# Feed-forward transposes by DMA in a four-layer forward and backward kernel

## The chip, the cores and the metric

The kernel runs on one core of a Trainium2 chip. The core has a matrix engine (TensorE, PE in the profile), a vector engine (VectorE, DVE), an activation engine (ScalarE, ACT), a general engine (GpSimd, POOL) and a queue engine that issues transfers (SyncE, SP). Sixteen DMA engines move data between the chip's memory (HBM) and the on-chip memory (SBUF). TensorE writes to PSUM, a small memory of eight banks. The metric is the device time of one execution in microseconds (us): 1243.02 us before, the median of three runs from 1242.3 to 1243.65.

## The reference

Two blocks are applied twice, in turn, to a sequence of 2048 rows of 512 numbers: a linear attention block A (32 heads of 16) and a gated feed-forward block B of width 1376. The kernel returns the output and the gradients of the input and of all weights.

```python
def _B_ref(x, w_gate, w_up, w_down):
    g = jnp.einsum("bsd,df->bsf", x, w_gate)
    u = jnp.einsum("bsd,df->bsf", x, w_up)
    h = _sigmoid(g) * u
    return jnp.einsum("bsf,fd->bsd", h, w_down)

x = A_x
x = x + _A_ref(_layernorm(x, axis=-1), A_wqkv, A_wo)
x = x + _B_ref(_layernorm(x, axis=-1), B_w_gate, B_w_up, B_w_down)
x = x + _A_ref(_layernorm(x, axis=-1), A_wqkv, A_wo)
x = x + _B_ref(_layernorm(x, axis=-1), B_w_gate, B_w_up, B_w_down)
...
_out, _vjp = jax.vjp(_f, A_x, A_wqkv, A_wo, B_w_gate, B_w_up, B_w_down)
_grads = _vjp(grad_out)
```

## The kernel before, in words

The sequence is cut into 16 tiles of 128 rows. The layers are numbered 0 to 3; 0 and 2 are A, 1 and 3 are B. Forward, `ab_fwd` goes over the 16 tiles and does, for each, the end of an A layer and the whole of the following B layer. Backward, `b_bwd_p1` goes over the tiles of layer 3, then of layer 1; the weight gradients are summed later, in `p2_gen`, from what these loops have stored in HBM.

Forward (`ab_fwd`). For a tile, `gu` computes one of three slices (512, 512 and 352 columns of the 1376) of g and u on TensorE, the sigmoid on ACT, the gated activation hh = u x sigmoid(g) on VectorE and the derivative factor on POOL. TensorE multiplies over the partition dimension, so hh has to stand with its 1376 columns on partitions before it can be multiplied with w_down: `transposes` does this with TensorE products against the identity matrix, 11 blocks of at most 128 columns for a tile, in three groups, and ACT copies each group from PSUM to hhT. `finish` multiplies hhT by w_down (11 matmuls) and adds the result to the residual. `finish` of a tile runs late in the next tile, `after` (LayerNorm of the next layer, or storing the output) two tiles later. At a tile's end SP issues the stores of hh and of the factors `ssd`; hh, hhT and ssd have two buffers each.

Backward (`b_bwd_p1`). For a tile, `dhh_mm` multiplies the gradient (transposed to gT by `gT_make`) by w_down transposed, in three slices. `dd_ops` multiplies each slice by the two factors of `ssd` on VectorE and so gives du and dg, both in the tile dd. They are transposed as in the forward pass: `transposes` makes 22 blocks in three groups on TensorE, and ACT copies them to ddT. `dh_mm` multiplies ddT by the transposed w_up and w_gate, 22 matmuls into one PSUM bank; `LnBwd` (`ln_begin`, `sums`, `add`) does the LayerNorm's backward step. `dh_mm` of a tile runs spread through the next tile, its LayerNorm steps in the one after. `store` writes du and dg to HBM from SP at the end of the tile: two transfers of 320 KB in rows of 512 bytes (sv_hdd) and one of 48 KB in rows of 192 bytes (sv_hdl). dd, ddT and ssd have two buffers each (in layer 3 the even tiles use buffers named pre_dd and pre_ssd); dhh_ps is in a PSUM pool of two banks.

Order. The instructions of TensorE, ACT, VectorE and POOL run in the order in which the program names them (`tc.manual_schedule`). SP issues transfers in order and waits, for each, for what it reads and for its target; a waiting transfer holds up those behind it. Transfers take eight completion slots in turn, so each also waits for the transfer eight before it. In layer 3 the loads of the operands of the weight gradients (p_a, 4 MB in eight transfers) are issued together after the load of ssd for tile 8.

The lines that the text speaks of: L860 to L866 are `gu`, L874 to L879 the forward `transposes`, L886 and L888 `finish`; L996 and L997 make gT, L1004 is `dhh_mm`, L1012 `dd_ops`, L1079 to L1083 the backward `transposes`, L1101 the load of ssd, L1113 `dh_mm`, L970 to L983 `LnBwd`, L1124 and L1126 `store`.

## Time and profile before

| What | Value |
|---|---|
| Median of three runs | 1243.02 us |
| Span of the profiled execution | 1244.3 us |
| TensorE busy | 1197.8 us, 96% of the span |
| VectorE, ACT, POOL busy | 726.8, 600.7, 258.1 us |
| DMA | 256.08 MB, on average 206 GB/s |
| Forward tile, layer 1 (two in a row) | 9.18 us each |
| Backward tile, layer 1 (two in a row) | 8.53 us each |
| dd L1012, idle until dhh_ps of L1004 | 150.6 us in 45 waits |

The page gives no time of the profiled execution beside its span; the span is 1.3 us above the median of the runs. In the profile a line of the groups gives count, busy time and mean length of the instructions of one source line; in the timeline each line is a start, a length, an engine, a line and what it wrote and read. Matmuls are pipelined, so that the length of one (219 ns for a 128x128 transpose) is more than the time after which the next one starts (some 56 ns in a group of eight). The table by stretches gives, for a window of time, its length, the busy time of PE, PEld, DVE, ACT and POOL with the number of instructions, the granted clock, the busy share of the 16 DMA engines and what they moved.

### The profile page before, as it was taken

Reading aid. Unit: us, or ns where it says so; the run is one execution under the profiler, and the core shown is the slowest. Engines: PE = TensorE matmul, PEld = TensorE weight load, DVE = VectorE, ACT = ScalarE, POOL = GpSimd, SP = SyncE. Lnnn points to the kernel's source line nnn. Section 1 sums busy time; section 2 is a strip of 40 time slices with the busy share of each in tenths; the row PEclk is TensorE's granted clock in tenths of the full one; section 3 lists DMA queues with packets and bytes.
Section 4 is the critical chain, followed back from the end, with each engine's and each line's share of the span. In section 5 each row is a group of like instructions: output and inputs, shape, how many; then the busy total and the mean of one; then the engine's idle time right before and its main releaser. Section 6 shows DMA issues by size and latency. Waiting matters only on the chain. (4 is left out here: it accounts for less than half of the span.)

```text
span 1244.3 us, 22419 instructions
## 1 busy us (share of the span) xinstructions
PE 1197.8 (96%) x8646; PEld 720.2 (58%) x8646; DVE 726.8 (58%) x1410; ACT 600.7 (48%) x1105; POOL 258.1 (21%) x467
## 2 busy tenths in 40 slices
PE   8989999998999999998989999999999979999998
PEld 4445555455555555554745567755555745567777
DVE  6778886777777456664956620056664956642211
ACT  5677777557676644444626621144545616610001
POOL 4246765105665300000100010000000101200000
PEclk8999999999999999998999999999999989999999
DMA  7934455435536877858644488687767666579774
GB/s 234 300 111 166 167 182 175 167 118 182 198 137 212 280 231 240 265 168 287 227 130 144 126 287 287 175 281 216 215 201 236 172 213 182 162 245 335 238 195 147
DMA packets 266203, 256.08 MB, mean 206 GB/s; under 512 B 43248, under 2 KB 250992, under 8 KB 261232
## 3 DMA queue, kind: packets, MB, share of 16 engines
q1 hardware_dynamic: 266096, 254.65, 64.4%
q8 instruction: 67, 1.10, 0.4%
q14 instruction: 40, 0.33, 0.1%
HBM read 135.69 MB, written 118.92 MB: 205 GB/s over the span
## 5 line engine op out<-in xcount | busy, mean ns | idle before, releaser
L1309 PE MATMUL p_ps<-p_set,p_a 128*128 128x256 bf16 (+1 forms) x1792 | 186.3, 263 | 0.0
L1012 DVE TENSOR_TENSOR dd<-dhh_ps,ssd 128x512 bf16<-128x512 f32 x144 | 82.6, 629 | 157.1 <-PE dhh_ps L1004 150.6
L1309 PEld LDWEIGHTS <-p_a 128*128 128x128 bf16 x1792 | 159.0, 98 | 18.8
L1081 ACT COPY ddT<-T_ps 128x1024 bf16<-128x1024 bf16 (+1 forms) x96 | 82.9, 868 | 126.2 <-PE T_ps L1079 126.2
L866 POOL TENSOR_TENSOR ssd_t<-hh_t,oms 128x512 bf16<-128x512 bf16 (+1 forms) x96 | 101.6, 1064 | 55.0 <-ACT out_t L212 40.9
L1113 PEld LDWEIGHTS <-ddT 128*128 128x128 bf16 (+1 forms) x704 | 66.4, 98 | 70.1 <-issue 1.4
L860 PEld LDWEIGHTS <-hT 128*128 128x128 bf16 x768 | 71.6, 98 | 58.8 <-issue 1.7
L978 POOL TENSOR_SCALAR ab<-c 128x2 f32<-128x2 f32 x64 | 12.3, 192 | 448.8 <-DVE junk L975 437.5
L1288 DVE TENSOR_TENSOR dw_stg<-p_ps,dw_stg 128x512 bf16<-128x512 f32 (+2 forms) x43 | 28.3, 660 | 112.0 <-PE p_ps L1309 78.3
L860 PE MATMUL g_ps<-wg,hT 128*128 128x512 bf16 (+1 forms) x384 | 90.9, 359 | 1.2 <-DVE hT L337 1.2
L860 PE MATMUL u_ps<-wu,hT 128*128 128x512 bf16 (+1 forms) x384 | 90.9, 359 | 0.0
L865 DVE TENSOR_TENSOR hh_t<-u_ps,ssd_t 128x512 bf16<-128x512 f32 (+1 forms) x96 | 61.0, 636 | 48.3 <-PE u_ps L860 28.4
L1004 PE MATMUL dhh_ps<-wdT,gT 128*128 128x512 bf16 x372 | 83.8, 362 | 2.7 <-ACT gT L997 2.7
L1113 PE MATMUL dh_ps<-wgT,ddT 128*128 128x512 bf16 (+1 forms) x352 | 86.2, 379 | 0.0
L1113 PE MATMUL dh_ps<-wuT,ddT 128*128 128x512 bf16 (+1 forms) x352 | 81.3, 379 | 1.2 <-ACT t_sb L970 1.2
L886 PE MATMUL y_ps<-wd,hhT 128*128 128x512 bf16 (+1 forms) x352 | 81.3, 379 | 0.6 <-DVE x L888 0.6
L1297 PE MATMUL p_ps<-p_a,p_set 128*128 128x512 bf16 (+1 forms) x352 | 81.6, 383 | 0.0
L862 ACT ACTIVATE ssd_t<-g_ps 128x512 bf16<-128x512 f32 (+1 forms) x96 | 53.2, 554 | 32.8 <-PE g_ps L860 32.6
L975 DVE SCALAR_TENSOR_TENSOR junk<-t_sb,h_ld 128x512 bf16<-128x512 f32 x64 | 44.0, 687 | 39.8 <-ACT t_sb L970 39.8
L970 ACT ACTIVATE t_sb<-dh_ps,rstd_all 128x512 f32<-128x512 f32 x64 | 44.0, 687 | 38.1 <-issue 20.3
L1568 ACT CAST fin_o<-sg_ps 128x512 bf16<-128x512 f32 x4 | 2.3, 586 | 122.1 <-PE sg_ps L1566 122.1
L1290 ACT CAST dw_stg<-p_ps 128x512 bf16<-128x512 f32 (+2 forms) x43 | 24.0, 561 | 76.5 <-PE p_ps L1309 48.4
(226 smaller groups left out, 2224.2 us busy)
## 6 DMA issues: line engine op xcount, KB each, us to landing
p_set<-sv_hdd SPq DMA_DIRECT2D x30, 1024.0 KB, 6.4
sv_ssd<-ssd_t SPq DMA_DIRECT2D x32, 688.0 KB, 3.4
ssd<-sv_ssd SPq DMA_DIRECT2D x24, 688.0 KB, 5.0
sv_hdd<-dd SPq DMA_DIRECT2D x48, 320.0 KB, 3.5
sv_hdd<-hh_t SPq DMA_DIRECT2D x32, 320.0 KB, 2.6
h_ld<-sv_h SPq DMA_DIRECT2D x32, 256.0 KB, 4.4
p_set<-sv_dqk SPq DMA_DIRECT2D x8, 1024.0 KB, 5.8
p_a<-sv_h SPq DMA_DIRECT2D x12, 512.0 KB, 6.2
```

The costliest lines, as they stand in the source:

```text
L860: nc.tensor.matmul(ps[:, 0:w], lhsT=hT[:, kc, :], rhs=w_sb[:, kc, c0:c0 + w], start=(kc == 0), stop=(kc == NDC - 1))
L862: nc.scalar.activation(ssd_t[:, 0, c0:c0 + w], g_ps[:, 0:w], ACT.Sigmoid)
L865: nc.vector.tensor_tensor(hh_t[:, c0:c0 + w], u_ps[:, 0:w], ssd_t[:, 0, c0:c0 + w], ALU.mult)
L866: nc.gpsimd.tensor_tensor(ssd_t[:, 1, c0:c0 + w], hh_t[:, c0:c0 + w], oms[:, 0:w], ALU.mult)
L886: nc.tensor.matmul(y_ps[:], lhsT=T["hhT"][0:r, fc, :], rhs=k.wd[0:r, fc, :], start=(fc == 0), stop=(fc == NFC - 1))
L970: k.nc.scalar.activation(self.t[:], dh_ps, ACT.Identity, scale=rstd_col, accum_out=self.c12[:, 0:1])
L1004: k.nc.tensor.matmul(ps[:, 0:w], lhsT=gT[:, jc, :], rhs=k.wdT[:, jc, c0:c0 + w], start=(jc == 0), stop=(jc == NDC - 1))
L1012: k.nc.vector.tensor_tensor(dd[:, a, c0:c0 + w], ps[:, 0:w], ssd[:, a, c0:c0 + w], ALU.mult)
L1081: nc.scalar.copy(ddT[:, :, fcs[0]:fcs[0] + nfull, :], tps[:, :, 0:nfull, :])
L1113: nc.tensor.matmul(T["dh"][:], lhsT=T["ddT"][0:r, a, fc, :], rhs=(k.wuT, k.wgT)[a][0:r, fc, :], start=(i == 0), stop=(i == 2 * NFC - 1))
L1297: nc.tensor.matmul(ps[0:r, :], lhsT=set_t[:, st, j * P:j * P + r], rhs=g_all[:, st, :], start=(st == 0), stop=(st == NST - 1))
L1309: nc.tensor.matmul(ps[:, icl * w:(icl + 1) * w], lhsT=h_all[:, st, ic * P:(ic + 1) * P], rhs=set_t[:, st, 0:w], start=(st == 0), stop=(st ...
```

## The change

Forward: the tile hh is widened from 1376 to 1408 columns (11 x 128), POOL fills the last 32 with zeros, and for tiles 0 to 14 one DMA issued by SP, ahead of the tile's stores, transposes the whole of hh into hhT. Tile 15 keeps its transposes on TensorE. `finish` moves to the middle of the tile two later, and `after` to three tiles later.

Backward: dd is widened in the same way. For tiles 2 to 14 one DMA issued by SP, after the last slice of du and dg, transposes both into ddT (22 blocks). Tiles 0, 1 and 15 stay on TensorE. ddT has three buffers. `dh_mm` of tiles 2 to 13 runs two tiles later; those of tiles 14 and 15 run after the last tile, and in tile 3 there is none. The stores of du and dg of a tile are issued by ACT, in the next tile, after the copy of gT. The eight loads of weight-gradient operands in layer 3 are issued one a tile from tile 6 on. The mask `bdmask` becomes bf16.

```diff
@@ -25,6 +25,7 @@
...
 FLAST = F - (NFC - 1) * P
+FP = NFC * P
 FSL = [(0, 512), (512, 512), (1024, F - 1024)]
@@ -218,7 +219,7 @@
...
                 else:
-                    k.pre["dd"] = pre.tile([P, 2, F], BF16, name="pre_dd")
+                    k.pre["dd"] = pre.tile([P, 2, FP], BF16, name="pre_dd")
                     for fs in range(2):
@@ -266,8 +267,18 @@
...
 
-        ops3 = []
-        b_bwd_p1(k, 3, lambda: ops3.extend(b_operands(k, R, 3)))
+        ops3, lds3 = [], []
+
+        def mid3(st):
+            if st == 6:
+                for src, nm in ((k.sv[3]["h"], "p2_a1"), (k.sv[3]["gbf"], "p2_a2")):
+                    t = R.big.tile([P, NST, D], BF16, name=nm)
+                    ops3.append(t)
+                    lds3.extend((t[:, b * NB:(b + 1) * NB, :], dram_batch(src, b)) for b in range(NST // NB))
+            if st >= 6 and lds3:
+                o, i = lds3.pop(0)
+                nc.sync.dma_start(out=o, in_=i)
+        b_bwd_p1(k, 3, mid3)
         prectx.close()
@@ -299,7 +310,7 @@
...
                             base=0, pattern=[[-1, P]], channel_multiplier=1)
-    bdmask = consts.tile([P, P], F32, name="bdmask")
+    bdmask = consts.tile([P, P], BF16, name="bdmask")
     nc.gpsimd.memset(bdmask[:], 1.0)
@@ -897,13 +908,19 @@
...
 
-        prev = None
+        def dma_T(T):
+            T["hhT"] = wide.tile([P, NFC, P], BF16, name="hhT")
+            nc.sync.dma_start(out=T["hhT"][:], in_=T["hh"][:], transpose=True)
+
+        Ts = []
         for st in range(NST):
+            last = st == NST - 1
             hT = ln.pop(st)
...
                      ssd=wide.tile([P, 2, F], BF16, name="ssd_t"),
-                     hh=wide.tile([P, F], BF16, name="hh_t"),
-                     hhT=wide.tile([P, NFC, P], BF16, name="hhT"))
+                     hh=wide.tile([P, FP], BF16, name="hh_t"))
+            nc.gpsimd.memset(T["hh"][:, F:FP], 0.0)
+            Ts.append(T)
             nfill = fill.share(st)
@@ -912,7 +929,6 @@
...
                 gu(T, hT, 1)
-                transposes(T, 0)
                 A.attn_y(2)
@@ -921,18 +937,25 @@
...
                 A.attn_y(st + YLAG)
-                after(st - 2)
+                after(st - 3)
                 if nfill > 0:
...
                 gu(T, hT, 1)
-                transposes(T, 0)
+                if last:
+                    T["hhT"] = wide.tile([P, NFC, P], BF16, name="hhT")
+                    transposes(T, 0)
+                if st >= 2:
+                    finish(Ts[st - 2])
                 ln.stage_T(st + 1)
...
                 nc.scalar.activation(k.tab[:], k.neg[:], ACT.Exp)
-            transposes(T, 1)
+            if last:
+                transposes(T, 1)
+            else:
+                dma_T(T)
             ln.apply(st + YLAG)
@@ -941,22 +964,23 @@
...
                 fill("t", "vector")
-            if prev is not None:
-                finish(prev)
+            if last:
+                finish(Ts[st - 1])
             A.front3(st + FLAG)
...
                 fill("t" * (nfill - 1), "scalar" if st % 2 else "vector")
-            transposes(T, 2)
+            if last:
+                transposes(T, 2)
             nc.sync.dma_start(out=sv["ssd"][rows(st), :, :], in_=T["ssd"][:])
...
             nc.sync.dma_start(out=sv["hdl"][0, :, st, :], in_=T["hh"][:, NG * GW:F])
-            prev = T
+        after(NST - 3)
         if out_cb is not None:
...
             last_cb(1)
-        finish(prev)
+        finish(T)
         if out_cb is not None:
@@ -1082,14 +1106,27 @@
...
 
-        def halved(st, nm, pool):
+        def halved(st, nm, pool, w=F):
             if not first:
-                return pool.tile([P, 2, F], BF16, name=nm)
+                return pool.tile([P, 2, w], BF16, name=nm)
             if st % 2:
-                return pool.tile([P, 2, F], BF16, name=nm, bufs=1)
+                return pool.tile([P, 2, w], BF16, name=nm, bufs=1)
             if st == 0:
                 return k.pre[nm]
-            return k.pre["pool"].tile([P, 2, F], BF16, name=f"pre_{nm}")
+            return k.pre["pool"].tile([P, 2, w], BF16, name=f"pre_{nm}")
+
+        def by_dma(st):
+            return 2 <= st < NST - 1
+
+        def dd_tiles(T):
+            T["dd"] = halved(T["st"], "dd", wide, FP)
+            T["ddT"] = wide.tile([P, 2, NFC, P], BF16, name="ddT", bufs=3)
+            if by_dma(T["st"]):
+                nc.gpsimd.memset(T["dd"][:, :, F:FP], 0.0)
+
+        def dma_T(T):
+            nc.sync.dma_start(out=T["ddT"][:].rearrange("p a c t -> p (a c) t"),
+                              in_=T["dd"][:].rearrange("p a f -> p (a f)"), transpose=True)
 
@@ -1099,9 +1136,9 @@
...
                 ins = nc.sync.dma_start(out=ssd[:], in_=sv["ssd"][rows(st), :, :])
-                if mid is not None and st == 8:
+                if mid is not None:
                     with tc.issue_after(ins.ins):
-                        mid()
+                        mid(st)
             LD[st] = (ssd, hld.get(st))
@@ -1121,13 +1158,9 @@
...
             for a in range(2):
-                nc.sync.dma_start(out=sv["hdd"][1 + a, :, :, st, :].rearrange("g p w -> p g w"),
-                                  in_=dd[:, a, 0:NG * GW].rearrange("p (g w) -> p g w", g=NG))
-            nc.sync.dma_start(out=sv["hdl"][1:3, :, st, :].rearrange("a p w -> p a w"), in_=dd[:, :, NG * GW:F])
-
-        def last_transposes(T):
-            transposes(T, 2)
-            store(T)
+                nc.scalar.dma_start(out=sv["hdd"][1 + a, :, :, st, :].rearrange("g p w -> p g w"),
+                                    in_=dd[:, a, 0:NG * GW].rearrange("p (g w) -> p g w", g=NG))
+            nc.scalar.dma_start(out=sv["hdl"][1:3, :, st, :].rearrange("a p w -> p a w"), in_=dd[:, :, NG * GW:F])
 
@@ -1135,45 +1168,59 @@
...
             gT_make(0)
-        p1 = p2 = None
         load(0)
+        Ts, done = [], []
         for st in range(NST):
...
             ssd, h_st = LD.pop(st)
-            T = dict(st=st, h=h_st, ssd=ssd, dd=halved(st, "dd", wide))
-            T["ddT"] = wide.tile([P, 2, NFC, P], BF16, name="ddT")
+            T = dict(st=st, h=h_st, ssd=ssd)
+            dd_tiles(T)
+            p1 = Ts[st - 1] if st else None
+            p = p1 if st in (1, 2) else Ts[st - 2] if st >= 4 else None
+            q = done[-1] if done and not done[-1].get("end") else None
             for fs in range(2):
...
                 if st == 1 and fs == 0:
-                    last_transposes(p1)
-            if p2 is not None:
-                p2["ln"].sums()
-            if p1 is not None:
-                dh_mm(p1, 0, NFC)
+                    transposes(p1, 2)
+            if q is not None:
+                q["ln"].sums()
+            if p is not None:
+                dh_mm(p, 0, NFC)
+            if not by_dma(st):
                 transposes(T, 0)
...
             gT_make(st + 1)
-            if p1 is None:
-                transposes(T, 0)
-            else:
-                dh_mm(p1, NFC, NFC + 5)
-            if p2 is not None:
-                p2["ln"].add()
-            transposes(T, 1)
             if p1 is not None:
-                dh_mm(p1, NFC + 5, 2 * NFC)
-                ln_begin(p1)
-                last_transposes(T)
-            p1, p2 = T, p1
-        p2["ln"].sums()
-        dh_mm(p1, 0, 2 * NFC)
-        p2["ln"].add()
-        ln_begin(p1)
-        p1["ln"].sums()
-        p1["ln"].add()
+                store(p1)
+            if by_dma(st):
+                dma_T(T)
+            if p is not None:
+                dh_mm(p, NFC, NFC + 5)
+            if q is not None:
+                q["ln"].add()
+                q["end"] = True
+            if not by_dma(st):
+                transposes(T, 1)
+            if p is not None:
+                dh_mm(p, NFC + 5, 2 * NFC)
+                ln_begin(p)
+                done.append(p)
+            if st and not by_dma(st):
+                transposes(T, 2)
+            Ts.append(T)
+        store(T)
+        for p in Ts[NST - 2:]:
+            q = done[-1]
+            q["ln"].sums()
+            dh_mm(p, 0, 2 * NFC)
+            q["ln"].add()
+            ln_begin(p)
+            done.append(p)
+        p["ln"].sums()
+        p["ln"].add()
 
```

## The prediction

> **What bounds the kernel now.** First the page's busy shares.
>
> ```profile
> PE 1197.8 (96%) x8646; PEld 720.2 (58%) x8646; DVE 726.8 (58%) x1410; ACT 600.7 (48%) x1105; POOL 258.1 (21%) x467
> ...
> DMA  7934455435536877858644488687767666579774
> ```
>
> TensorE is busy nearly always; no other engine is. So work taken off TensorE is worth its own length wherever nothing else becomes later than TensorE. The second line says where that is doubtful: the DMA engines stand at 0.4 to 0.5 in the forward feed-forward (slices 3 to 13) and at 0.6 to 0.9 in the backward one (slices 15 to 18, 28 to 30).
>
> Second, the timeline of one backward tile (layer 1), in order of start (start, length, engine, line).
>
> ```profile
> 904.42 0.61 PE L1079 MATMUL T_ps<-ident,dd 128*128 128x128 bf16 x8
> 904.87 0.76 PE L1004 MATMUL dhh_ps<-wdT,gT 128*128 128x352 bf16 x4
> 905.47 0.39 PE L996 MATMUL gT_ps<-ident,gstage 128*128 128x128 bf16 x4
> 906.03 0.59 ACT L997 COPY gT<-gT_ps 128x512 bf16<-128x512 bf16 x1
> 906.77 0.61 PE L1079 MATMUL T_ps<-ident,dd 128*128 128x128 bf16 x8
> 907.21 1.46 PE L1113 MATMUL dh_ps<-wgT,ddT 128*128 128x512 bf16 x6
> 908.51 0.50 PE L1079 MATMUL T_ps<-ident,dd 128*128 128x128 bf16 x6
> 908.85 1.89 PE L1004 MATMUL dhh_ps<-wdT,gT 128*128 128x512 bf16 x8
> ```
>
> Read the starts, not the lengths, which overlap: the three transpose groups hold TensorE 0.45 + 0.44 + 0.34 = 1.23 us.
>
> Third, the busy time by stretch: two forward tiles, two backward tiles, then three short stretches inside backward tiles (last two columns: DMA share, GB/s).
>
> ```profile
> 125.00:134.18 9.18, 9.18 (x63) 4.98 (x62) 7.78 (x15) 6.67 (x13) 6.18 (x11) 1.00 0.64 216
> 134.18:143.36 9.18, 9.18 (x64) 4.96 (x62) 8.02 (x15) 6.71 (x13) 6.25 (x11) 1.00 0.45 160
> ...
> 896.34:904.87 8.53, 8.53 (x64) 4.76 (x61) 5.46 (x10) 4.03 (x7) 0.77 (x3) 1.00 0.72 218
> 904.87:913.40 8.53, 8.53 (x63) 4.78 (x61) 5.46 (x10) 4.03 (x7) 0.77 (x3) 1.00 0.70 211
> ```
>
> ```profile
> 898.55:900.75 2.20, 2.20 (x21) 1.25 (x18) 0.95 (x2) 1.53 (x2) 0.00 (x0) 1.00 1.01 281
> ...
> 910.60:911.20 0.60, 0.60 (x4) 0.27 (x3) 0.60 (x3) 0.00 (x0) 0.00 (x0) 1.00 0.97 139
> 911.60:913.40 1.80, 1.80 (x16) 1.03 (x14) 1.40 (x4) 0.00 (x0) 0.31 (x2) 1.00 0.96 364
> ```
>
> A backward tile keeps the DMA engines full for 0.71 x 8.53 = 6.06 us; a forward tile for 0.55 x 9.18 = 5.0 us. Full engines move 281 GB/s with the stores in rows of 512 bytes, about 139 while the 192-byte rows of sv_hdl go, 364 with the 5,504-byte rows of ssd.
>
> Fourth, issue to landing (us, last column).
>
> ```profile
> sv_ssd<-ssd_t SPq DMA_DIRECT2D x32, 688.0 KB, 3.4
> ssd<-sv_ssd SPq DMA_DIRECT2D x24, 688.0 KB, 5.0
> sv_hdd<-dd SPq DMA_DIRECT2D x48, 320.0 KB, 3.5
> sv_hdd<-hh_t SPq DMA_DIRECT2D x32, 320.0 KB, 2.6
> ```
>
> The same size takes 0.9 to 1.6 us longer in the backward tiles than in the forward ones.
>
> **Forward transposes.** Eleven of the 11 x 15 x 2 per tile go: the groups of 4, 4 and 3 hold TensorE 0.22 + 0.22 + 0.17 = 0.61 us a tile, 30 tiles: 18.4 us. Three ACT copies a tile go too, beside TensorE. Added: one DMA of 128x1408 (352 KB) on SP, ahead of the tile's own stores. Its result is used a tile and a half later, about 14 us, against 2.6 to 5 us for such transfers; engine time 5.0 + 1.5 = 6.5 of 8.57 us. VectorE has 7.9 us of work in that tile: if its 0.67 us of slack were gone, the gain would be too. A POOL fill of 32 columns waits until the buffer's stores of two tiles before have landed; behind it are prod and the tiny LayerNorm steps, on an engine busy 6.2 of 9.18 us: nothing taken. finish and after run a tile later; their work is the same and the last tile takes two. Taken: -18.4; ends 0 and -18.4.
>
> **Backward transposes.** 22 per tile on 13 tiles of two layers go, so TensorE's tile is 8.53 - 1.23 = 7.30 us, and 2.97 us of ACT copies go. The question is what else allows 7.30.
>
> Engines: the added DMA carries 22x128x128 bf16 = 721 KB. No row shows a transposing DMA. The bounds are the three paces above: 2.0 us of full engines at 364 GB/s, 5.2 us at 139. Its blocks are 128 elements wide, 256 bytes, between the 192-byte and the 512-byte rows; at 281 it is 2.6 us, and I take 3.0 us, a little dearer than the 512-byte row. Then a layer-1 tile needs 6.06 + 3.0 = 9.06 us of DMA engines, more than the 8.53 us it takes now.
> The Trainium skill (DMA: Bandwidth & Descriptors, Latency and other measured facts) gives 261 GB/s for one DMA-transpose kernel; by that figure the transpose would be an estimated 2.76 us, the layer-1 tile 8.82 us and the sum below about 1249; no run here shows it yet.
>
> Stores: those of tile st move from SP in tile st to ACT in tile st+1, after the gT copy. du and dg have two buffers, so the first product of tile st+2 waits for them. The ring: gT copy ends 1.75 us after the third dhh group starts (904.87 to 906.62); the third store is issued 0.93 us later (an SP row for two issues) and lands 3.2 us after that (sv_hdl row); the two products of slice 0 take 1.24 us (four in 2.48); only then has the next third dhh group its PSUM buffer. Sum 7.1 us, with the handovers about 7.3: no slack against 7.30. The transpose of the tile is issued at the same time as these stores, and they share engines; with the 1.6 us between the two 688 KB rows the ring is 8.9 us. Behind the waiting VectorE product are the rest of du/dg, LayerNorm's sums and the transpose's source; behind ACT's stores (which also wait for an earlier DMA's slot) are the read of dh and the next gT copy; behind SP's transpose, which waits for slice 2, is the load of ssd two tiles on; behind POOL's pad fill the LayerNorm scalars and the gradient cast.
>
> So a layer-1 tile: 9.05 us, 13 x 0.52 = +6.8 us. Layer 3: now 0.67 x 8.5 = 5.7 us of DMA engines (window 445 to 453.5), so five tiles follow the ring, 8.9 us: 5 x 0.37 = +1.9. In tiles 6 to 13 one 512 KB load each is issued, 1.8 us at 285 GB/s, so 5.7 + 3.0 + 1.8 = 10.5: 8 x 1.97 = +15.8. Before, these loads came in a burst that cost TensorE 1.3 us (38.67 of 40 in 480 to 520), which is got back: +16.4 for the layer.
>
> Lag: tile 3 has no dh product and one more (22 x 0.216 = 4.76 us) stands after the last tile. If the ring or the engines set the tile, tile 3 is hardly shorter. Between 0 and +4.8 a layer I take 3.0: +6.
>
> Mask in bf16: four products in all, nothing; range 0 to -1.
>
> **Sum.** The profiled execution has a span of 1244.3 us, 1.3 above the median of the runs; no row gives more around it. -18.4 + 6.8 + 16.4 + 6 = +10.8: 1255.1, less 1.3: about 1253 us. With the transpose at 5.2 us a layer-1 tile is 11.3, layer 3's are 10.9 and 12.7: +35 + 45 + 6 - 18: about 1311. At 2.0 us the engines need 8.06 and 9.5 us, ring 7.7: -6 + 3 + 6 - 18: 1228.
>
> **Rivals.** *The transposes hide (faster).* Engines hold queues full only when asked; layer-1 tiles have 2.5 us of idle engine each. If the transposing DMA is cheap and the stores have landed before it starts (ring 7.5), both layers gain about 13 x 1.0, the lag costs 3 a layer, so 1243 - 18 - 26 + 6 = about 1205; halfway, with a tile of 8.0, 1220. It decides below about 2.4 us of full engines per transpose (l-1 tile at 8.5). For it: VectorE reaches slice 2 after slices 0, 1 and the sums, so the transpose comes 1 us or so after the stores. Against: 28% idle is what is left between bursts.
>
> *The transpose is far dearer* than its bytes, in the engines or in SP's issue: from 6 us a tile the backward tiles are 12 us or more, 26 x 3.5 = +91, 1243 - 18 + 91 + 6 = about 1320. For it: 192-byte rows at half the pace. Against: one such DMA is 128 full partitions.
> The Trainium skill (VectorE: DVE Perf Modes, The three transpose paths) lists 1309 ns for a 128x128 block by DMA; were 22 blocks to go one after another, an estimated 29 us a tile, the kernel would end beyond 1700; the trace bears this out nowhere, one chance in forty within the 0.13 below.
>
> *The forward does not gain* (VectorE at 7.9 of 8.57 us): 18 us worse than the forecast, 1271.
>
> **How the numbers follow.** About 0.2% (2.5 us) is what a measurement here can tell. Slower as forecast 0.37 (own range 1246 to 1285), dearer transposes 0.13, forward without gain 0.05; hidden or half hidden 0.39; 0.06 within 0.2%, between the two. The range leaves out a tenth on each side: below 1210, above 1305.
>
> **What would show it.** the transposes of du and dg (now L1079) down from 704 to 132 matmuls; dd L1012 waiting for sv_hdd or sv_hdl instead of for dhh_ps; DMA share above 0.9 in the backward tiles; forward tiles near 8.57 us; backward tiles near 9 and 10.5. Backward tiles under 8.2 us or transposes landing in under 4 us make the forecast wrong; transposes landing after 10 us make it too low.

## The result, and the profile after

The changed kernel takes 1374.69 us (median of three runs, 1371.96 to 1375.78) against 1243.02: a ratio of 1.105, 95% interval 1.102 to 1.108. The forecast was 1253 us, range 1210 to 1305. The direction was right, the size far off.

The page of the changed kernel: TensorE's busy line, the granted clock, the DMA share.

```profile
PE 1204.8 (88%) x7744; PEld 681.9 (50%) x7744; DVE 718.9 (52%) x1410; ACT 482.6 (35%) x881; POOL 268.6 (20%) x525
...
PEclk9999988999999999999899999999989999999999
DMA  7744454643554698999965539789999666649875
```

902 matmuls are gone (8646 to 7744), yet TensorE is "busy" 7 us longer and 8 points less of the span: it waits, and in the slices where it waits its matmuls run longer. Two stretches stand out (slices counted from 0): in 3 to 13 (forward feed-forward) the DMA share is no higher than before although a transfer was added; in 16 to 19 and 27 to 30 (backward) it is at 9.

To see where the 129.8 us of span went (1374.1 against 1244.3), I cut each trace at four marks: the last feed-forward addition of layer 1 and of layer 3 (`x<-y_ps,x` on VectorE), and ACT's read of the last dh of layer 3 and of layer 1 (`t_sb<-dh_ps`). The stage called "backward 1" starts where layer 2's backward pass reads its last dh. All other stages take 7.1 us less together. The same stages take 441.4 to 449.2 us in the six kernels here that leave them as they were, and 439.2 here, so most of the 7.1 us lies within what they vary by.

| Stage, us | before | after | difference | forecast, same stage |
|---|---|---|---|---|
| forward 1 | 224.7 | 272.7 | +48.0 | -9.2 |
| forward 3 | 208.8 | 242.4 | +33.6 | -9.2 |
| backward 3 | 137.0 | 161.7 | +24.7 | +19.4 |
| backward 1 | 227.5 | 258.1 | +30.6 | +9.8 |

So 81.6 us of the loss come from the forward pass, where the forecast had a gain of 18.4.

**Forward.** The stretches of two tiles of layer 1 (columns as in the prediction's table of stretches; the last three are granted clock, DMA share, GB/s):

```profile
145.88:159.49 13.61, 10.42 (x53) 4.83 (x51) 7.64 (x15) 4.97 (x9) 6.80 (x11) 0.88 0.54 159
159.49:173.10 13.61, 10.42 (x52) 4.84 (x51) 7.63 (x15) 5.01 (x10) 6.78 (x11) 0.88 0.54 168
```

A tile takes 13.61 us instead of 9.18, TensorE works 10.42 of it, and the granted clock is 0.88 where it was 1.00. No engine and no DMA is full. The timeline of the first of these tiles shows the gap (in brackets: idle before, and what ended it):

```profile
151.81 1.25 PE L897 MATMUL y_ps<-wd,hhT 128*128 128x512 bf16 x5
...
153.71 0.76 PE L871 MATMUL u_ps<-wu,hT 128*128 128x352 bf16 x4
...
156.56 1.04 DVE L795 TENSOR_TENSOR pqnstage<-pq_all,rden_all 128x512 bf16<-128x512 bf16 x1
...
157.66 0.40 PE L341 MATMUL ln_tp<-ident,pqnstage 128*128 128x128 bf16 x4 [3.19 <-DVE pqnstage L795]
157.89 1.57 PE L871 MATMUL g_ps<-wg,hT 128*128 128x512 bf16 x4
```

and the same place of the kernel before:

```profile
128.63 2.54 PE L886 MATMUL y_ps<-wd,hhT 128*128 128x512 bf16 x11
130.05 0.90 DVE L784 TENSOR_TENSOR pqnstage<-pq_all,rden_all 128x512 bf16<-128x512 bf16 x1
131.00 0.23 PEld L330 LDWEIGHTS <-pqnstage 128*128 128x128 bf16 x4 [0.33 <-DVE pqnstage L784]
```

`front2` makes `pqnstage` on VectorE (a sum over `prod`, a reciprocal, a product), and `front3` transposes it on TensorE. Before, the 11 matmuls of `finish`, 2.54 us, stood between the two and covered that chain; what was left was a wait of 0.33 us of the weight load. The change moves `finish` to the middle of the tile. It ends at 153.06, the g and u products behind it at 154.47, and `pqnstage` is there at 157.60: TensorE stands idle for 3.19 us in this tile, and for 69.7 us in 27 such waits over both layers. The rest of the 4.4 us is slower matmuls: 10.42 us of work where 9.18 - 0.61 = 8.57 was left, at the clock of 0.88; directly after the gap a group of 4 takes 1.57 us, 4.5 us later 1.03. (3.19 of idling and 1.85 of slower work, less the 0.61 taken away, are the 4.4.)

**Backward.** DMA issues of the changed kernel (size where the profile has it, then median us from issue to landing):

```profile
ssd<-sv_ssd SPq DMA_DIRECT2D x24, 688.0 KB, 5.0
sv_hdd<-dd ACTq DMA_DIRECT2D x48, 320.0 KB, 4.3
...
sv_hdl<-dd ACTq DMA_DIRECT2D x24, 48.0 KB, 5.8
...
hhT<-hh_t SPq DMA_TRANSPOSE x30, 3.5
...
ddT<-dd SPq DMA_TRANSPOSE x19, 7.6
```

The forward transposes land after 3.5 us, and nobody waits for them. The backward ones take 7.6, and sv_hdl, the last store of a tile, takes 5.8 where it took 3.2 before the change. The timeline of the changed kernel in layer 1:

```profile
1001.86 0.59 ACT L1021 COPY gT<-gT_ps 128x512 bf16<-128x512 bf16 x1 [6.69 <-PE gT_ps L1020]
...
1002.93 0.76 ACTq L1163 DMA_DIRECT2D sv_hdl<-dd  x1
...
1003.75 5.58 SPq L1128 DMA_TRANSPOSE ddT<-dd  x1
...
1008.14 2.48 DVE L1036 TENSOR_TENSOR dd<-dhh_ps,ssd 128x512 bf16<-128x512 f32 x4 [3.44 <-DMA sv_hdl<-dd]
...
1010.70 0.59 ACT L1021 COPY gT<-gT_ps 128x512 bf16<-128x512 bf16 x1 [4.15 <-PE gT_ps L1020]
```

This is the prediction's ring, link by link: from the gT copy 1.07 us to the issue of sv_hdl, 5.21 to the product that waited for its landing, 2.56 to the next gT copy: 8.84 us, where 7.3 was worked out for stores that land undisturbed. One turn later the landing takes 8.2 us and the tile 13.95. Tiles 2 to 14 average 10.08 us in layer 1 and 9.99 in layer 3. The waits of the whole span (engine, line, releaser: us in total, times, longest):

```profile
DVE dd L1036 <- DMA sv_hdl<-dd: 94.0, 18, 9.3
...
PE ln_tp L341 <- DVE pqnstage L795: 69.7, 27, 3.2
...
DVE pre_dd L1036 <- DMA sv_hdl<-pre_dd: 35.9, 7, 8.5
```

Forward wait and backward wait are both in this list; both were small in the kernel before (`pqnstage`: 4.4 us in 3 waits, sv_hdl: 3.6 us in one).

### The profile page after: what moved, and what is told of

Same layout as the page of the kernel before. It is cut to its first block, busy times and chain, and to the rows that moved or that the text cites. A ratio compares the mean times of both kernels' runs of the same rounds, so it can differ in the third digit from the quotient of the medians.

```text
span 1374.1 us, 20635 instructions
## 1 busy us (share of the span) xinstructions
PE 1204.8 (88%) x7744; PEld 681.9 (50%) x7744; DVE 718.9 (52%) x1410; ACT 482.6 (35%) x881; POOL 268.6 (20%) x525
## 5 line engine op out<-in xcount | busy, mean ns | idle before, releaser
L1356 PEld LDWEIGHTS <-p_a 128*128 128x128 bf16 x1792 | 159.9, 98 | 19.4
L1028 PE MATMUL dhh_ps<-wdT,gT 128*128 128x512 bf16 x372 | 88.2, 375 | 58.7 <-DVE dd L1036 38.6
L1150 PEld LDWEIGHTS <-ddT 128*128 128x128 bf16 (+1 forms) x704 | 71.7, 104 | 91.3 <-issue 24.7
L871 PEld LDWEIGHTS <-hT 128*128 128x128 bf16 x768 | 76.2, 104 | 73.7 <-issue 23.9
L871 PE MATMUL u_ps<-wu,hT 128*128 128x512 bf16 (+1 forms) x384 | 107.4, 409 | 0.0
L871 PE MATMUL g_ps<-wg,hT 128*128 128x512 bf16 (+1 forms) x384 | 99.1, 384 | 2.4 <-DVE hT L348 2.4
L1150 PE MATMUL dh_ps<-wgT,ddT 128*128 128x512 bf16 (+1 forms) x352 | 96.6, 429 | 0.0
L1028 PEld LDWEIGHTS <-gT 128*128 128x128 bf16 x372 | 36.7, 101 | 102.8 <-issue 62.5
L1021 ACT COPY gT<-gT_ps 128x512 bf16<-128x512 bf16 x31 | 18.2, 587 | 166.1 <-PE gT_ps L1020 166.1
L341 PE MATMUL ln_tp<-ident,pqnstage 128*128 128x128 bf16 x128 | 12.9, 224 | 69.7 <-DVE pqnstage L795 69.7
```

What stands on the lines that cost most here:

```text
L871: nc.tensor.matmul(ps[:, 0:w], lhsT=hT[:, kc, :], rhs=w_sb[:, kc, c0:c0 + w], start=(kc == 0), stop=(kc == NDC - 1))
L1028: k.nc.tensor.matmul(ps[:, 0:w], lhsT=gT[:, jc, :], rhs=k.wdT[:, jc, c0:c0 + w], start=(jc == 0), stop=(jc == NDC - 1))
L1150: nc.tensor.matmul(T["dh"][:], lhsT=T["ddT"][0:r, a, fc, :], rhs=(k.wuT, k.wgT)[a][0:r, fc, :], start=(i == 0), stop=(i == 2 * NFC - 1))
L1356: nc.tensor.matmul(ps[:, icl * w:(icl + 1) * w], lhsT=h_all[:, st, ic * P:(ic + 1) * P], rhs=set_t[:, st, 0:w], start=(st == 0), stop=(st ...
```

## The experiments

Two questions. Forward: does the order of `finish`, or the added DMA, cost 82 us? Backward: late stores, SP's queue held by the transposes, or the DMA engines? "The changed kernel" is meant where nothing else is said. A time without a range is that of one run. Stages that a kernel does not alter still differ between such runs: forward 1 takes 220.1 to 224.8 us in four kernels with the forward pass of before, and backward 1 225.1 to 227.5 in three with its backward pass; forward 3 and backward 3 stay within 0.5.

### Forward: the order, the DMA, and each alone

`finish` of two tiles back put again between `front2` and `front3`, all else as changed:

```
-                if st >= 2:
-                    finish(Ts[st - 2])
                 ln.stage_T(st + 1)
...
+            if st >= 2:
+                finish(Ts[st - 2])
...
             A.front3(st + FLAG)
```

> The changed kernel with one move in the forward pass: finish (w_down product, 11 matmuls, still of the tile two before) stands again between the normalising of pq (front2, VectorE) and its transposes (front3, TensorE), as in the kernel before; the DMA transposes stay. Theory ORDER (TensorE stands idle until VectorE's pqn because finish no longer lies between them, and its clock drops): forward tiles fall from 13.6 and 12.1 us to 8.6 to 9.2 us, the wait of ln_tp on pqnstage goes from 70 us to under 10, the total from 1374 to about 1280 us. Rival TRANSFER (the transposing DMAs themselves hold up the forward pass, by their landing or by the engines they fill): forward tiles stay above 12 us and the total at about 1370 us.

The kernel before, with its TensorE transposes, and only `finish(prev)` moved ahead of `ln.stage_T`:

> The kernel before with one move and no DMA transpose: finish of the tile before stands in the middle of the tile (after the second slice), no longer between front2 and front3. ORDER: forward tiles go from 9.2 and 9.4 us to 12 us or more, the total from 1243 to about 1310 us (a little less than in the changed kernel's forward pass, since two groups of transposes still fill some of the gap). TRANSFER: forward tiles stay within 0.3 us of 9.2 and the total at 1243 us.

The kernel before with the forward DMA transposes, `finish` and `after` left in their old place:

```
...
-            transposes(T, 1)
+            if last:
+                transposes(T, 1)
+            else:
+                nc.sync.dma_start(out=T["hhT"][:], in_=T["hh"][:], transpose=True)
...
```

> The kernel before with the forward DMA transposes alone (tiles 0 to 14), finish of the tile before in its old place; the backward pass as before. ORDER: forward tiles lose the 0.61 us of their transposes, 8.6 and 8.8 us, total about 1225 us (18 us less than before). TRANSFER: forward tiles 10 us or more, total 1260 us or more.

| Kernel | forward 1 | forward 3 | total |
|---|---|---|---|
| before | 224.7 | 208.8 | 1243.0 |
| changed | 272.7 | 242.4 | 1374.7 |
| changed, `finish` back | 227.6 | 208.4 | 1296.05 |
| before, order alone | 275.0 | 253.1 | 1341.97 |
| before, forward DMA alone | 219.8 | 205.1 | 1231.55 |

The order by itself, with no DMA transpose at all, costs 94.6 us of the two stages; putting it back in the changed kernel returns 79.1. The wait on `pqnstage` follows: with the order alone it is nearly that of the changed kernel,

```profile
PE ln_tp L330 <- DVE pqnstage L784: 64.5, 27, 3.0
```

and it falls to 13.7 us with `finish` back and 9.1 with the DMA alone. So the forward loss is the order's, and the DMA is a gain.

The gain is smaller than the 18.4 us of TensorE time taken away: the total falls by 10.8 us, 1231.55 (1229.99 to 1231.75) against 1242.34, ratio 0.9915 (0.9896 to 0.9935), and the two forward stages show 8.6 us of it. The tiles tell it more safely than forward 1 does: they go from 9.2 to 8.96 us in layer 1 and from 9.4 to 8.91 in layer 3, not by 0.61. The waits of this kernel show one place where the rest is:

```profile
PE ln_tp L331 <- DVE pqnstage L785: 9.1, 15, 2.1
```

Twelve waits more than before at the very place that the order opened wide: VectorE's chain is nearly late already.

The same run prices a transpose. Stretches of 8 tiles, first of the kernel before, then of the one with forward DMA alone:

```profile
125.00:197.90 72.90, 72.90 (x491) 39.66 (x490) 63.04 (x119) 53.41 (x104) 49.32 (x79) 1.00 0.49 173
336.00:411.30 75.30, 75.25 (x529) 42.44 (x528) 55.14 (x106) 52.69 (x108) 44.73 (x57) 1.00 0.55 189
```

```profile
123.00:195.00 72.00, 69.91 (x410) 35.28 (x409) 62.82 (x121) 41.07 (x73) 50.66 (x90) 1.00 0.72 218
330.00:401.30 71.30, 70.81 (x438) 36.74 (x437) 55.47 (x108) 39.91 (x76) 44.09 (x64) 1.00 0.82 239
```

0.72 x 72.0 - 0.49 x 72.9 = 16.1 us of full engines for 8 transposes, 0.82 x 71.3 - 0.55 x 75.3 = 17.1 in layer 3: 2.0 to 2.1 us for 352 KB, so 4.0 to 4.2 for the 704 KB of a backward tile. The packets of the transposes, 256 bytes each, say the same by themselves: their times add up to 1.93 us of the 16 engines for a forward transpose in this run and to 4.27 for a backward one in the changed kernel. A packet's time may hold some waiting for other transfers, so this is nearer to an upper end. The Trainium skill (DMA: Bandwidth & Descriptors, Latency and other measured facts) gives 261 GB/s, measured on one kernel whose middle dimension was not contiguous, and about 350 to 400 for the contiguous case; by the 261 the 704 KB would take an estimated 2.76 us. Here it is some 170 to 190 GB/s, and the measurement decides.

### Backward: one suspect at a time

Each of these starts from the changed kernel, so the forward stages stay near 274 and 242. The factors' loads left out for tiles 4 to 15; then a third dd buffer in layer 1; then only du by DMA.

> The changed kernel without the loads of ssd for tiles 4 to 15 of both backward layers (left out: these tiles use the factors of tiles 2 and 3, so the gradients are of other numbers); all else as in the changed kernel. Theory ENGINES (the 16 DMA engines are full in the backward layers, share 1.00 and 1.03): 688 KB a tile less is some 2.0 us of engines, so the backward tiles fall from about 10.2 to about 8.3 us and each layer's stage from 131 to 134 us to about 108 to 112 us; total about 1325 to 1330 us. Rival RING (the stores of du and dg, issued a tile later and beside the transpose, come back too late for the two buffers of dd): the stores and the transposes are untouched, so the stages stay within 5 us of 131 to 134 us and VectorE still waits some 130 us for sv_hdl.

> The changed kernel with three buffers instead of two for dd in layer 1 only (layer 3 as it was). RING: in layer 1 the wait of VectorE and POOL for sv_hdl vanishes and the layer-1 stage falls from 258 to about 240 us, layer 3 stays at 162; total about 1356 us. ENGINES: layer 1 stays within 5 us of 258, total about 1372 us.

> The changed kernel with only du transposed by DMA in the backward tiles (361 KB instead of 721 KB) and dg on TensorE (11 blocks, 0.61 us a tile). ENGINES: half of the transpose's engine time, some 2.2 us a tile, goes, so tiles fall from 10.2 to about 8.3 us, stages from 162 and 258 to about 140 and 235 us, total about 1330 us. RING: stores share engines with a transfer half as long, landing about 1.5 us earlier, stages about 145 and 240 us. The two differ little here; the run gives the price of the transposed bytes.

The backward transposes left out (ddT of these tiles is then one buffer of zeros):

```
         def dma_T(T):
+            return
...
```

> The changed kernel with the backward transposing DMAs left out (dh of tiles 2 to 14 is computed from zeros, so the gradients behind it are of other numbers); stores still issued by ACT a tile late, two dd buffers. It prices the ring alone: with landings of 3.2 to 3.5 us the ring is 7.3 us, as long as TensorE's 7.30 us, so tiles of 7.3 to 7.6 us, stages of about 127 and 222 us and hardly a wait for sv_hdl. If the ring is late by itself, tiles of 8.5 us or more and a wait for sv_hdl above 50 us remain.

The stores given back to SP in their own tile, ahead of the transpose; and the same without the transposes:

```
-                nc.scalar.dma_start(out=sv["hdd"][1 + a, :, :, st, :].rearrange("g p w -> p g w"),
+                nc.sync.dma_start(out=sv["hdd"][1 + a, :, :, st, :].rearrange("g p w -> p g w"),
...
-            if p1 is not None:
-                store(p1)
+            store(T)
...
```

> The changed kernel with the stores of du and dg issued again by SP in their own tile, ahead of the tile's transpose. RING (two dd buffers, stores issued a tile late and beside the transpose): VectorE's wait for sv_hdl, 130 us in the changed kernel, goes to under 20 us; the backward stage of layer 3 falls from 162 to about 145 us or less, that of layer 1 (with the end of the attention layer before it) from 258 to about 240; total about 1340 us. ENGINES (DMA engines full whatever the order): the wait only changes its name (ddT or ssd late), stages stay within 5 us, total about 1370 us.

> The changed kernel without the backward transposing DMAs (dh of tiles 2 to 14 computed from zeros) and with the stores by SP in their own tile. Against the run that left out the transposes alone (stages 155.8 and 244.9 us), it takes away the late stores. QUEUE: nothing is left that is later than TensorE, tiles 7.3 to 7.6 us, stages about 128 and 219 us, total about 1320 us. If something else in the changed order (the dh product two tiles later, the pad fills) costs time, stages stay above 140 and 230 us.

The kernel before, with nothing but its stores moved to ACT and to the next tile, after the gT copy:

> The kernel before with only the stores of du and dg issued by ACT in the next tile, after the gT copy; all transposes on TensorE. QUEUE: with two dd buffers and the 48 KB store landing 5.3 us after its issue (as it did without transposes beside it) the ring is some 9.4 us, longer than TensorE's 8.53 us: tiles of about 9.3 us, stages 137 and 227.5 go to about 148 and 239 us, total about 1265 us, with a wait of VectorE for sv_hdl of 10 us or more. ENGINES or TRANSFER: without the transposes the late stores are hidden, tiles 8.53 us, total 1243 us.

| Kernel | backward 3 | backward 1 | total | what VectorE's dd products wait for |
|---|---|---|---|---|
| before | 137.0 | 227.5 | 1243.0 | dhh_ps |
| changed | 161.7 | 258.1 | 1374.7 | sv_hdl, 129.9 us |
| no factor loads | 152.0 | 241.4 | 1351.68 | sv_hdl, 108.6 |
| third dd buffer in layer 1 | 163.4 | 242.2 | 1360.69 | sv_hdl, 69.2; ssd, 39.0 |
| du alone by DMA | 155.4 | 254.2 | 1368.78 | sv_hdl, 114.5 |
| no transposes | 155.8 | 244.9 | 1361.62 | sv_hdl, 109.6 |
| stores in own tile | 155.0 | 241.0 | 1352.2 | ssd, 102.3 |
| no transposes, stores in own tile | 122.6 | 213.7 | 1296.41 | dhh_ps |
| before, late stores alone | 159.7 | 243.2 | 1280.38 | sv_hdl, 125.3 |

Against what was expected: the third buffer and the run without transposes came out as the reading by the ring had it, the late stores cost even more than it said, and the last but one was faster than expected. No factor loads and stores in own tile fell between the two readings; du alone stayed above both.

Read the last two against each other. With neither late stores nor transposes every tile from the seventh on takes exactly 7.30 us, the value worked out for TensorE. With late stores alone, and every transpose still on TensorE, the kernel before loses 22.7 and 15.7 us. Its timeline:

```profile
887.15 0.59 ACT L997 COPY gT<-gT_ps 128x512 bf16<-128x512 bf16 x1
...
888.06 0.64 ACTq L1126 DMA_DIRECT2D sv_hdl<-dd  x1
...
894.16 2.48 DVE L1012 TENSOR_TENSOR dd<-dhh_ps,ssd 128x512 bf16<-128x512 f32 x4 [4.97 <-DMA sv_hdl<-dd]
...
896.90 0.59 ACT L997 COPY gT<-gT_ps 128x512 bf16<-128x512 bf16 x1
```

The same ring, 9.75 us, over the 8.53 that TensorE needs, with the DMA engines at a share of 0.65. So full engines are not needed for this loss, and "the engines alone" falls. But "the late stores alone" falls as well: given back to SP (stores in own tile) the stages stay at 155.0 and 241.0, with the wait moved to ssd, whose load stands behind the transpose in SP's queue:

```profile
DVE dd L1036 <- DMA ssd<-sv_ssd: 75.3, 18, 6.7
```

(and 27.0 us more in layer 3's other buffer). Taking one cause away leaves the other; only both together free the tile.

### Late, or on ACT?

The kernel before again, its stores written at the late place but issued by SP; then issued by ACT, but at the old place.

> The kernel before, with the stores of du and dg one tile later, at the place that the changed kernel gives them, but issued by SP. Before: stages 137.0 (layer 3) and 227.5 (layer 1), total 1243.0; the same lateness with ACT issuing: 159.7, 243.2 and 1280.38, its stores landing after 5.5 us. Theory, ACT's queue makes the loss: on SP the stores land after 3.2 to 3.5 us, the ring (1.75 us to the gT copy, 0.93 to issue, 3.2 to land, 1.24 for two products) is 7.1 us, inside 8.53; stages within 3 us of 137 and 227.5, total 1240 to 1248, VectorE waits under 10 us for the stores. Rival, lateness makes it: issued so late the stores meet the other transfers whichever queue they are on and land after 5 us or more, stages above 150 and 238, total over 1265.

> The kernel before with the stores of du and dg issued by ACT in their own tile, after the tile's last copy to ddT. Before: stages 137.0 (layer 3) and 227.5 (layer 1). ACT issuing them a tile later: 159.7 and 243.2, total 1280.38. Theory lateness: here the stores leave some 2.7 us after the last product, against 0.6 on SP and 6 to 9 on ACT a tile later, and have about 7.6 us to land before their buffer is written again, against landings of 5.5; stages within 3 us of 137.0 and 227.5, total 1240 to 1248. Rival, ACT's queue: transfers on it land late or hold up ACT's copies behind them whenever they are issued; stages above 150 and 236, total over 1262.

The first gave 143.5 and 227.3, 1250.27 us (1239.76 for the kernel before beside it), outside both expectations, and it did not test what it was meant to. SP's order is not the written one: the trace shows the stores leaving 0.55 us behind the start of the tile's last product, in their own tile.

```profile
884.01 0.96 DVE L1012 TENSOR_TENSOR dd<-dhh_ps,ssd 128x352 bf16<-128x352 f32 x2 [1.19 <-PE dhh_ps L1004]
...
884.56 0.36 SPq L1124 DMA_DIRECT2D sv_hdd<-dd  x1
```

So layer 1 was unchanged; the 6.5 us of layer 3 are one tile of 16.03 us at the burst of its eight loads. The second gave 138.7 and 230.8, 1241.53 us beside 1242.77: with ACT's queue but without the lateness nothing of the 38 us is left but 1.7 and 3.3 (the second 0.3 outside what was expected). So the late place makes the loss, not ACT's queue as such; ACT keeps that place because it issues a transfer only when its own written order has got there.

### What the transposes cost when nothing else is late

`finish` back in its old place, stores by SP in their own tile, and the factors' loads issued by ACT so that they no longer stand behind a transpose:

> The changed kernel with three waits taken away: forward, finish of the tile before in its old place; backward, the stores of du and dg by SP in their own tile ahead of the transpose, and the loads of ssd issued by ACT, so that they do not stand behind the transpose on SP. The transposing DMAs of both directions stay. Theory QUEUE (the backward loss comes from what stands behind what: first the late stores with two dd buffers, and with these gone the ssd load behind a transpose that holds SP for 5 us): backward tiles fall to 7.5 to 8.3 us, stages from 137 and 227.5 in the kernel before to 128 to 138 and 218 to 228 us, total 1215 to 1232 us. Rival ENGINES (the transposed bytes fill the DMA engines): tiles of 9 us or more, stages of 150 and 236 or more, total 1255 us or more.

1270.67 us (1268.23 to 1271.81), ratio 1.022 (1.019 to 1.025) to 1243.49; stages 160.0 and 243.8, in the range of the rival. The waits on stores and factors are all but gone, and dd and ddT now wait for the transposes themselves, which land after 8.0 us (20.2 at most). Most tiles take 7.3 us, between them some of 12 to 23. Two readings were left: SP's queue, which a transpose holds for 5.9 us of 7.3, or the DMA engines. Three kernels, each from this one: the stores issued by POOL; dg's half of each transpose issued by ACT; and transposes only in the even tiles 2 to 14. In the first and the third the loads of layer 3 also stand behind the stores.

> The kernel with all three cleared (forward finish in its old place, stores in their own tile, factors' loads issued by ACT), but the stores of du and dg issued by POOL, so that SP's queue holds little besides the transposing DMA. That kernel took 1270.67 us, its layer-3 backward stage 160.0 and its layer-1 one 243.8; without any transpose and with own-tile stores the two were 122.6 and 213.7. Theory SP's issue time: a transpose holds SP 5.9 us and the stores some 1.6 more, over a tile's 7.30; without the stores SP keeps up, dd and ddT are free in time, most tiles are 7.3 to 7.8 us, the stages near 130 and 219, the total near 1216. Rival DMA engines: the transpose needs about 4.4 us of them beside 6.1 us of other transfers, 10.5 us a layer-1 tile whoever issues them; stages stay within 5 us of 160 and 244, the total 1262 to 1280, transposes still land after 8 us or more.

> The kernel with all three cleared, but du transposed by SP's queue and dg by ACT's, each 360 KB; the traffic is the same. That kernel: layer-3 stage 160.0, layer-1 stage 243.8, total 1270.67. Theory SP's issue time: a transpose of half the size held SP 2.2 us (median) in the kernel with du alone, so SP has some 5 us of a tile instead of 8 to 9, tiles fall to 7.3 to 8, the stages to about 132 and 220, the total to about 1220. Theory DMA engines: the windows of the kernel with forward transposes alone give 2.0 us of engines for 360 KB (0.72 of 72.0 us against 0.49 of 72.9, 8 tiles), so 4.05 for both halves beside 6.06 us of other transfers, 10.1 us a layer-1 tile on whichever queue; stages stay within 8 us of 160 and 244, the total 1260 to 1285.

> The kernel with all three cleared, but with DMA transposes in the even backward tiles 2 to 14 alone (7 a layer, the others on TensorE), and the 512 KB loads of layer 3 behind the tile's stores on SP. Two tiles need 7.30 + 8.53 = 15.83 us of TensorE and, in layer 1, 2 x 6.1 + 4.4 = 16.6 us of DMA engines. Theory engines or SP's issue time, whichever, at half the load: the spikes of 12 to 23 us go, tiles average 8.0 to 8.3, stages near 131 and 222 (before 137.0 and 227.5), total 1216 to 1226, below the 1231.55 of the kernel with the forward transposes alone. Rival: each transpose delays what stands around it by itself, whatever the rate (a landing of 8 us or more in its own tile holds the next use of ddT or dd): stages lie halfway, near 148 and 233, total 1240 to 1250, and the backward transposes are worth nothing at any rate.

The first missed both expectations by far: 1438.33 us, stages 228.7 and 342.0. The transposes there land after 16.0 us (median, 48.0 at most). The stretch in which two of them were under way, behind POOL's stores:

```profile
486.50:519.00 32.50, 1.07 (x5) 0.29 (x3) 0.00 (x0) 0.21 (x2) 0.15 (x1) 0.56 1.25 85
```

Nothing works for 32.5 us, and the engines count as more than full while they move 85 GB/s. To see whether POOL's queue is slow by itself, its stores without any transpose:

> The changed kernel with the backward transposing DMAs left out (their results are zeros) and the stores of du and dg issued in their own tile, by POOL. With SP issuing them so, the stages were 122.6 and 213.7 and the total 1296.41. Theory POOL's queue is slow by itself: its stores land after 10 us as they did beside the transposes, dd has two buffers, tiles of 8.5 to 10 us, stages over 135 and 228. Rival, slow only beside a transposing DMA: stages within 5 us of 122.6 and 213.7, landings of 4 to 6 us.

Stages 122.7 and 215.6, landings of 6.2 us, total 1295.81: no. In these runs it is slow only beside the backward transposing DMAs. Why, these runs do not show.

With the two halves on two queues SP is held 1.5 us by its half and ACT 2.3 by the other, the halves land after 3.9 and 5.7 us, yet the stages are 165.8 and 254.2, the total 1290.09: SP's time falls as the cause. The engines' reading came nearer, but put the layer-1 stage at 244, 10.2 us below the measured one, and the total at 1285 at most; part of that is a new wait, ACT's `t_sb` behind its transpose of dg (46.8 us in 9 waits on dd).

With every other tile, the tiles of layer 1 did what was worked out: from the sixth on they alternate between 7.78 and 8.05 us, 15.83 the pair, TensorE's own time. The stretches of layer 1, first of this kernel and then of the one with a transpose in every tile:

```profile
832.00:895.00 63.00, 63.00 (x392) 33.12 (x391) 41.91 (x79) 21.35 (x40) 6.54 (x20) 1.00 1.02 267
```

```profile
840.00:950.00 110.00, 92.35 (x446) 42.12 (x444) 63.73 (x117) 16.36 (x36) 10.27 (x34) 0.92 1.08 266
```

(The share adds up the times of all packets, so it can pass 1.) At half the rate the engines are just full (1.02) and TensorE never waits; at the full rate they are more than full (1.08) and move no more (266 GB/s against 267), and TensorE works 92 of 110 us. Without transposes and with own-tile stores the same kind of stretch has 0.89. By the price above, 6.06 + 4.05 = 10.1 us of engines a layer-1 tile against 7.30 of TensorE; two tiles with one transpose need 16.2 against 15.83. This reading is the nearest to all these runs but the one with POOL's stores. Its 10.1 us is not a hard bound, though: with a transpose in every tile, tiles 2 to 14 of layer 1 average 8.79 us, and 26.6 us instead of 22.0 follow the last gT copy. That a transpose is also slow to land for another reason is not excluded.

Still the gain is small: 1229.01 us (1224.86 to 1235.19), ratio 0.990 (0.985 to 0.994), where 1216 to 1226 was expected. Layer 1's loop gains 7.3 us, and the lag gives 5.1 back behind the last tile (22.0 us from the last gT copy to the end of the stage, 16.9 before): 225.7 against 227.5. Layer 3 is 143.1, a miss: the same lag costs 5.1 there, and two tiles of 12.4 and 14.0 us, in which VectorE waits for a transpose to land, use up what the others gain. The second of them:

```profile
537.92 2.48 DVE L1033 TENSOR_TENSOR pre_dd<-dhh_ps,pre_ssd 128x512 bf16<-128x512 f32 x4 [7.36 <-DMA ddT<-pre_dd]
```

So a last kernel leaves layer 3's backward loop as it was before, without the lag, and keeps every other tile in layer 1:

> Forward transposes by DMA with the forward work in its old place; the layer-3 backward loop with TensorE transposes alone and without the lag; in layer 1 the even tiles 2 to 14 by DMA, with the lag. Layer 1 as in the kernel with every other tile: tiles alternate 7.78 and 8.05, 7.3 us gained over the loop, 5.1 lost behind the last tile (22.0 us from the last gT copy to the end of the stage against 16.9), so its stage is near 225.7; layer 3 back at 137. Theory that both readings add up: total 1229.0 - 6 = 1221 to 1227. Rival, that layer 3's 143.1 came from its loads in the middle or ACT's loads of the factors and not from the transposes: layer 3 stays above 140 and the total within 1226 to 1234.

Layer 3 is back at 137.5, as the theory had it: without the lag its 5.1 us are gone, and without transposes the two waits. (Its loads also go out in one burst again; that was not taken apart.) Layer 1 has 227.8, with 11.4 us at its first tile, and the total is 1230.98 (1228.90 to 1232.42), ratio 0.990 (0.988 to 0.992): inside the rival's range and not the theory's. The three kernels that are faster than before, 1229.0, 1231.0 and 1231.55, can't be told apart by their ratios: the forward transposes alone bring as much, and the backward ones add nothing that shows.

## Why the prediction was wrong

**Forward, -18.4: the step that failed.** The prediction said: "finish and after run a tile later; their work is the same", and costed the move at nothing. It cost 82 us net. Its work is the same, but its place was the cover of VectorE's chain to `pqnstage`. For the pad fill the prediction named what stands behind it; for `finish` it did not name what its place covers, though the trace of the kernel before had it: 2.54 us of matmuls that end at 131.17, with `pqnstage` done at 130.95. With the place kept, the rest of the step was right in kind: the transposes land long before they are used (3.5 us), and the gain is 10.8 of the 18.4 us (8.6 of them in the two forward stages); at least part of the rest is VectorE's chain, as the rival "the forward does not gain" had it. Measured engine time of a forward transpose: 1.9 to 2.1 us, not 1.5.

**Engines, 3.0 us a backward transpose:** mis-sized. It takes 4.0 to 4.3, within the two ends (2.0 and 5.2). Its 256-byte blocks were taken nearer to the 512-byte row than to the 192-byte one; the time of a packet, interpolated between the rows (192 bytes at 139 GB/s are 1.38 ns of all 16 engines, 512 at 281 are 1.82, so 256 take 1.47, 174 GB/s), would have given 4.1 us. A layer-1 tile was to need 9.05 us; it took 10.08, but late stores alone, with every transpose on TensorE, also bring it to 9.84.

**Stores, 7.3 to 8.9 us:** the ring is real, link by link, and the mis-sized link is the landing of sv_hdl: 3.2 us was taken from stores that leave in their own tile; a tile late it took 5.8 and 6.0 in the changed kernel and 5.5 and 6.9 with late stores alone (medians of its two groups), and 8 and more in single tiles. The contended ring of 8.9 us was near the single turns shown (8.84, 9.75), but not near the worst (13.95), and the prediction let it set five tiles of layer 3 only. That it costs 38 us over the two layers by itself, without any added DMA, was not seen. The load of ssd behind SP's transpose was named and given no price; SP is held 4.4 to 9.0 us by each, and with the stores in their own tile that load is what 102.3 us of waits are for.

**Layer 3, 8.9 and 10.5 us:** average 9.9 forecast, 9.99 measured. That agreement is partly luck: late stores alone, with every transpose on TensorE, give 10.3 there. **Lag, +3 a layer:** 5.1 measured behind the last tile with every other tile; in the changed kernel the stretch behind the last gT copy is 10.8 us longer in layer 1 and 6.8 in layer 3; in layer 1 VectorE waits 6.6 us for sv_hdl there, so the ring holds in it too. Loops and tails together: +17.8 and +6.8 in layer 3, +19.5 and +10.8 in layer 1 (and 0.3 ahead of it).

Of the 119 us between the forecast's +10.8 and the measured +129.8, the forward step is 100.0, the backward ones 26.1, and the other stages -7.1. So "slower" came true in good part by a stage for which a gain was forecast. Of the rivals, "the transposes hide" holds at every other tile only. "Far dearer", from 6 us a transpose and with tiles of 12, was not the case either (tiles of 10): its 1320 was nearer to the time, but for a wrong reason. Even a kernel with the forward term as forecast would have been slower: the backward stages alone lost 55 us. Two slips of the prediction change little: 1255.1 less 1.3 is 1253.8, and the DMA digits of slices 3 to 13 run from 3 to 8, not from 4 to 5.

## What to carry to other kernels

Before a block of work is moved at "no cost", look in the trace at what waits next on the engine that it leaves: the producer that was hidden behind it comes out (here 3.0 to 3.2 us a time at most), and with it the clock may fall (here to 0.88). A transfer that an in-order compute engine issues leaves when that engine's written order gets there, not when its data are ready; count the buffer's ring from there, with landing times of that moment. When two causes each suffice, taking one away shows little: only the run without both, here 7.30 us a tile, tells what each is worth.

## What was not expected of the hardware

- A transposing DMA holds its issuing queue: 1.26 to 2.10 us for 352 KB, 4.4 to 9.0 for 704 KB in the changed kernel, and up to 30 us while POOL's stores were under way. Size alone does not set it: 352 KB took 1.49 to 3.06 us in the backward tiles with du alone.
- POOL's stores and transposing DMAs slow each other far beyond their bytes: 85 GB/s at a share of 1.25, landings up to 48 us, where POOL's stores without transposes land after 6 to 7 us and transposes beside SP's stores after 8 (medians).
- Gaps of up to 3.2 us a tile on TensorE came with a granted clock of 0.88 (0.87 with the order alone); with `finish` back the forward stretch has 1.00.
- The Trainium skill (DMA: Bandwidth & Descriptors, Issuing engines are not separate DMA queues) says that issuing on several engines only saves the sequencer's time. The split of the transposes over two queues agrees (no stage gained). Moving the stores to ACT also cost, 22.7 and 15.7 us of stage, where ACT's order put them late; in their own tile it cost 1.7 and 3.3.
